# Visits of P.V over four blocks of keys with ten half tiles of P, and an order of work counted with shorter engine occupations

## The chip, the cores and the metric

The kernel runs on one core of one Trainium2 chip. The metric is the time of one execution in microseconds (us); below, a time without a unit is in us. Engines are named as in the profile: PE is TensorE (PEld its weight loads), DVE VectorE, ACT ScalarE, POOL GpSimd, SP the queue from which nearly all transfers are issued. Most executions of one kernel agree within 0.3%.

## The reference

`x` has 2048 rows of 576 values. The result is `x + s * g`, where both branches start from the normalized rows:

```python
xn = _layernorm(x)
# s: attention, 32 heads of 18 values
qkv = (xn @ wqkv).reshape(1, 2048, 3, 32, 18)
scores = einsum("bhqd,bhkd->bhqk", q, k) * 18 ** -0.5
p = softmax(scores)
s = einsum("bhqk,bhkd->bhqd", p, v).reshape(1, 2048, 576) @ wo
# g: a bilinear feed-forward part, 4608 wide, then silu
g = silu(((xn @ w_gate) * (xn @ w_up)) @ w_down)
return x + s * g
```

Everything is float32 outside; the kernel splits a float32 operand into a high and a low part and multiplies these (three products for one).

## The kernel before

There are three stages. The **prologue** (until about 205 us of the span) normalizes x, turns it into columns `xc`, and computes q, k (`qk_block`, nine blocks of 128 columns of `wqkv`) and v. The weights of a pair of blocks come by `w_load` into a raw tile and are split by `w_split`: for each block a piece of four 128-row chunks and a piece of the last 64 rows, each one ACT copy (L119) and one POOL subtraction (L121). The **end** (from about 2628 us) multiplies the attention's result by `wo` and joins the two branches, 16 tiles of 128 rows.

In between lies the **main stage**, where attention and the feed-forward part run together on PE. Most of its matmuls use half of PE's rows: the program has two streams, r = 0 in rows 0 to 63 and r = 1 in rows 64 to 127, and a matmul of one half runs beside one of the other. PE takes them in the order of the program. In each stream stand:

- `gu_op` (L630): the up (r = 0) and gate (r = 1) products of the feed-forward part, 27 matmuls of 512 columns for each 128 of its 4608 columns and each 512 rows of x: 72 units of two groups in each half, 7776 in all.
- `down_op` (L658): the product with `w_down`, 288 columns wide; 72 units of 4 times 12 matmuls in each half, 6912 in all.
- `a_item` (L534, r = 0): scores of one head for 128 queries by 512 keys; DVE takes the largest of each row (L536). 64 for each head, 2048 in all.
- `b_item` (L567, r = 1, at the end r = 0 too): the same scores again, turned over (128 keys by 512 queries) and less the maximum; ACT writes their exponentials (L569) into half of a tile `pt`. 64 for each head; the four of one block of 128 keys fill two tiles `pt` (two "half tiles" of P, 128 x 1024 each).

The product of P with V (`pv_group`, L578) uses all rows of PE and 32 of its columns for each of four matmuls. It is done in **visits**: PE leaves the two streams, does the four matmuls of each block of keys that is due, and goes back to the streams. What a visit summed in PSUM is copied by ACT (L582) on a head's first visit, and added to `oc` by DVE (L584) on the others. A head has 16 blocks of keys. After the last, `finish` turns `oc` (L594; for the last four heads PE does it, L608) and divides.

The order in which all this is written is made by a planner in Python (`order`, L973, with `visit`, `small`, `a_next`, `b_next`, `can_go`, `late`): it keeps a clock for each half of PE and a time for DVE, ACT, each PSUM bank and the transfers, and always writes down what its clocks say can go next. Its costs: 0.229 for a matmul of 512 columns, 0.131 for one of 288, 0.70 for a DVE reduction, 0.60 for an exponential, 0.858 for a block in a visit, 0.1 ahead of a visit and 0.22 behind it. A visit is asked for when `need` blocks are due (three while scores are left), and `b_ready` holds back scores that the tiles `pt` (8) have no room for (`AHEAD` = 7). `pace` spreads the scores over the stage's planned length `span`. The chip doesn't know of these numbers: it runs the written order, each engine in its own order, with semaphores where one needs another's result.

Of the kernel before, what the change touches and what calls it, by code (L numbers as in the profile page):

```python
# [40 lines left out]
def kernel(  # L41
# [51 lines left out]
    jp = consts.tile([128, 128], I32, name="jp")  # L93
    nc.gpsimd.iota(jp, pattern=[[1, 128]], base=0, channel_multiplier=-1)
    ident = consts.tile([128, 128], FT, name="ident")
    nc.vector.tensor_scalar(ident, jp, 0.0, None, op0=OP.is_equal)
# [4 lines left out]
    def w_load(srcs):  # L101

        raw = wpool.tile([128, 2, 5, 128], FT, name="wraw", bufs=2)[:, 0:len(srcs)]
        for i, (m, c0) in enumerate(srcs):
            nc.sync.dma_start(raw[:, i, 0:4, :],
                              m[0:512, c0:c0 + 128].rearrange("(k p) c -> p k c", p=128))
            for b in (0, 64):
                nc.sync.dma_start(raw[b:b + 64, i, 4, :], m[512:576, c0:c0 + 128])
        return raw

    def w_split(raw, n, pool=None):

        if pool:
            w = pool.tile([128, n, 10, 128], FR, name=f"wq{n}")
        else:
            w = wpool.tile([128, 2, 10, 128], FR, name="wgu", bufs=2)

        def piece(i, d, n, src):
            nc.scalar.activation(w[:, i, d:d + n, :], raw[:, i, src:src + n, :], AF.Copy)  # L119
            low = 4 + d if d < 8 else 9  # L120
            nc.gpsimd.tensor_tensor(w[:, i, low:low + n, :], raw[:, i, src:src + n, :],  # L121
                                    w[:, i, d:d + n, :].bitcast(FT), op=OP.subtract)

        return w, [(piece, a) for i in range(n) for a in ((i, 0, 4, 0), (i, 8, 1, 4))]
# [142 lines left out]
    ep = early.enter_context(tc.tile_pool(name="early", bufs=1, side="right"))  # L267
    vp = vstack.enter_context(tc.tile_pool(name="vp", bufs=1))
# [61 lines left out]
    def qk_block(b, c):  # L330
        w = wq[b // 2][:, b % 2]
        p = bank("a" if nqk[0] % 2 else "b", 2)
        nqk[0] += 1
        for n, (a, e) in enumerate(PAIRS):
            nc.tensor.matmul(p, w[:, a, :], xcs[c][:, e, :], start=n == 0,  # L335
                             stop=n == len(PAIRS) - 1)
# [61 lines left out]

    def w_now(i):
# [35 lines left out]
    for c in range(NCH):  # L435
# [25 lines left out]
        if c == 2:  # L461
            w_now(4)
# [690 lines left out]
```

## Time and profile before

| | us |
|---|---|
| median of 3 runs | 2706.16 (2703.46 to 2708.2) |
| the profiled execution, its time | 2705.18 |
| the profiled execution, its span | 2703.4 |
| PE busy in the span | 2654.6 |
| PE weight loads busy | 2130.2 |
| DVE busy | 1975.9 |
| ACT busy | 1489.9 |
| POOL busy | 452.4 |

The span runs from the first to the last instruction; the execution's time has 1.8 us more around it. Busy times of engines overlap, and a PE that is busy need not be busy in both halves of its rows. In the chain of work that ended last, PE holds 90%, transfers 5%, DVE 3%. The lines of the page and of the trace on which the argument rests are shown with it, below. In a row of the timeline stand the start, the duration, the engine, the line, the operation, the tiles written and read, the matmul's part of the array or the shapes, how many instructions the row holds, and in brackets the idle time before it with what ended it.

### The profile page before, as it was taken

What the parts mean: (1) busy time and instruction counts of PE and PEld (TensorE: products, weight loads), DVE (VectorE), ACT (ScalarE), POOL (GpSimd) and SP (SyncE); (2) the same over time, 40 slices, a digit from 0 to 9 for tenths busy, and PEclk for the clock granted to TensorE, in tenths of its full rate; (3) what the DMA queues carried; (4) which work ended last, traced back from release to release, by engine and by line L of the source; (5) the groups of instructions that cost most, each with busy time, mean ns of one, the idle gap of its engine ahead of it and who ended that gap; (6) DMA issues with size and microseconds to landing.
All of it is one profiled execution on the core that took longest, in us unless ns stands there. A gap on an engine that the chain in (4) does not pass through costs nothing.

```text
span 2703.4 us, 59095 instructions
## 1 busy us (share of the span) xinstructions
PE 2654.6 (98%) x24456; PEld 2130.2 (79%) x24456; DVE 1975.9 (73%) x3446; ACT 1489.9 (55%) x2731; POOL 452.4 (17%) x419
## 2 busy tenths in 40 slices
PE   7999999999999999999999999999999999999999
PEld 6899877777778787877778777777777787877769
DVE  7208777777777787877778788777778777877726
ACT  4222666666665555555555555555555555555662
POOL 3113333333311011111001101100001001100005
PEclk9999999999999999999999999999999999999999
DMA  6799888888875555666575555565676565565436
GB/s 214 225 286 263 244 224 217 220 221 214 233 201 168 164 164 176 181 203 181 163 196 165 171 164 160 168 176 164 151 199 159 167 167 174 160 177 164 137 138 209
DMA packets 212821, 508.63 MB, mean 188 GB/s; under 512 B 71112, under 2 KB 130888, under 8 KB 179016
## 3 DMA queue, kind: packets, MB, share of 16 engines
q1 hardware_dynamic: 209512, 493.64, 64.8%
q0 software_dynamic: 3040, 11.21, 1.1%
q8 instruction: 192, 3.15, 0.5%
q14 instruction: 77, 0.63, 0.1%
HBM read 314.05 MB, written 109.97 MB: 157 GB/s over the span
## 4 chain that ended last, share of the span: by engine, by line
PE 90%; DMA 5%; DVE 3%; issue 1%; ACT 1%; POOL 0%; SPq 0%; POOLq 0%; ACTq 0%; DVEq 0%
PE pg L630 32%; PE pg L578 16%; PE pg L658 14%; PE pa L534 12%; PE pb L567 8%; PE pg L1110 2%; PE pg L389 2%; PE pa L335 2%; DMA wd<-swd 2%; PE pb L335 2%; DMA wgu<-swg 1%; DVE mx L536 1%; DMA wop<-in_A_wo_dram 1%; DMA hs<-hs 1%; DVE xn L297 0%
## 5 line engine op out<-in xcount | busy, mean ns | idle before, releaser
L630 PE MATMUL pg<-xc,wgu 64*128 64x512 f32 x7776 | 1652.7, 392 | 6.9 <-DMA wgu<-swg 3.6
L569 ACT ACTIVATE pt<-pb 128x512 f32<-128x512 f32 x2048 | 1176.7, 596 | 727.8 <-PE pb L567 572.7
L536 DVE TENSOR_REDUCE mx<-pa 128x1 f32<-128x512 f32 x2048 | 1363.4, 685 | 181.0 <-PE pa L534 73.7
L630 PEld LDWEIGHTS pg<-xc,wgu 64*128 64x128 f32 x7776 | 1178.9, 186 | 59.8 <-issue 4.2
L658 PE MATMUL pg<-wd,hs 64*128 64x288 f32 x6816 | 1040.0, 293 | 4.5 <-DMA wd<-swd 3.4
L658 PEld LDWEIGHTS pg<-wd,hs 64*128 64x128 f32 x6816 | 973.4, 186 | 23.6 <-issue 5.2
L567 PE MATMUL pb<-qs,ks 56*128 56x512 f32 x2048 | 806.7, 409 | 7.4 <-ACT pt L569 6.5
L534 PE MATMUL pa<-ks,qs 54*128 54x512 f32 x2048 | 798.9, 403 | 0.1
L534 PEld LDWEIGHTS pa<-ks,qs 54*128 54x128 f32 x2048 | 365.6, 185 | 160.1 <-issue 125.8
L578 PE MATMUL pg<-pt,vt 128*32 128x512 f32 x4096 | 481.2, 599 | 3.7 <-DVE us L642 1.7
L646 POOL TENSOR_TENSOR hs<-us,hs 128x512 fp32r<-128x512 f32 x144 | 186.0, 1292 | 1775.6 <-ACT hs L645 1665.0
L567 PEld LDWEIGHTS pb<-qs,ks 56*128 56x128 f32 x2048 | 365.2, 185 | 25.8 <-ACT pt L569 13.1
L584 DVE TENSOR_TENSOR oc<-oc,pg 128x512 f32<-128x512 f32 x160 | 110.0, 688 | 334.3 <-PE pg L578 334.0
L578 PEld LDWEIGHTS pg<-pt,vt 128*32 128x32 f32 x4096 | 113.8, 109 | 250.9 <-issue 234.8
L686 DVE TENSOR_TENSOR acc<-acc,pg 128x288 f32<-128x288 f32 x544 | 239.9, 446 | 46.5 <-PE pg L658 38.9
L645 ACT ACTIVATE hs<-us 128x512 fp32r<-128x512 f32 x144 | 91.0, 632 | 160.7 <-DVE us L642 158.6
L210 POOL TENSOR_TENSOR wgu<-wraw,wgu 128x384 fp32r<-128x384 f32 x108 | 108.3, 1014 | 154.7 <-ACT wgu L209 147.3
L642 DVE TENSOR_TENSOR us<-pg,us 128x512 f32<-128x512 f32 x144 | 98.5, 684 | 5.8 <-PE pg L630 2.4
L635 ACT ACTIVATE us<-pg 128x512 f32<-128x512 f32 x144 | 85.6, 595 | 19.0 <-PE pg L630 16.8
L241 POOL TENSOR_TENSOR wd<-draw,wd 128x576 fp32r<-128x576 f32 x36 | 51.3, 1428 | 102.3 <-ACT wd L240 86.9
L339 DVE TENSOR_TENSOR hl<-pb,hl 128x512 fp32r<-128x512 f32 x18 | 12.4, 690 | 73.2 <-ACT hl L338 73.2
L582 ACT ACTIVATE oc<-pg 128x512 f32<-128x512 f32 x32 | 19.1, 598 | 84.7 <-PE pg L578 84.7
(102 smaller groups left out, 1071.7 us busy)
## 6 DMA issues: line engine op xcount, KB each, us to landing
wgu<-swg SPq DMA_DIRECT2D x102, 1152.0 KB
hs<-hs SPq DMA_DIRECT2D x288, 256.0 KB
wd<-swd SPq DMA_DIRECT2D x50, 1152.0 KB
swg<-wgu SPq DMA_DIRECT2D x36, 1152.0 KB
qs<-sqk SPq DMA_DIRECT2D x192, 144.0 KB
ks<-sqk SPq DMA_DIRECT2D x192, 144.0 KB
swd<-wd SPq DMA_DIRECT2D x18, 1152.0 KB
sqk<-hl SPq DMA_DIRECT2D x32, 512.0 KB
```

The source lines that it names most:

```text
L210: nc.gpsimd.tensor_tensor(w[:, 9 + b:12 + b, :], raw[:, b:b + 3, :], w[:, b:b + 3, :].bitcast(FT), op=OP.subtract)
L335: nc.tensor.matmul(p, w[:, a, :], xcs[c][:, e, :], start=n == 0, stop=n == len(PAIRS) - 1)
L534: nc.tensor.matmul(p, q[rows, t * 128:(t + 1) * 128], k[rows, c * 512:(c + 1) * 512], start=True, stop=True)
L536: nc.vector.tensor_reduce(mx[h][:, t, c:c + 1], p, axis=AX.X, op=OP.max)
L567: nc.tensor.matmul(p, k[rows, t * 128:(t + 1) * 128], q[rows, c * 512:(c + 1) * 512], start=True, stop=True)
L569: nc.scalar.activation(pt[t, c // 2][:, c % 2, :], p, AF.Exp, scale=scale)
L578: nc.tensor.matmul(p[32 * c:32 * c + 32, :], vt[h // 2][:, t, 6 * (h % 2):6 * (h % 2) + 32], pt[t, c // 2][:, c % 2, :], start=t == ts[0], ...
L584: nc.vector.tensor_tensor(oc[h], oc[h], p, op=OP.add)
L630: nc.tensor.matmul(ps, gw[n][half[r], a, :], xg[i][half[r], e, :], start=k == 0, stop=k == len(TERMS) - 1)
L646: nc.gpsimd.tensor_tensor(hj[:, 1, :], h32, hj[:, 0, :].bitcast(FT), op=OP.subtract)
L658: nc.tensor.matmul(ps[:, 0:HALF], hs[u][half[r], k, j, a, s * 128:(s + 1) * 128], dw[u][half[r], k, j, e, :], start=n == 0, stop=n == len( ...
L686: nc.vector.tensor_tensor(a, a, ps[:, 0:HALF], op=OP.add)
```

## The change

It has three parts.

**The main stage.** There are ten tiles `pt` (`HALVES`), and a visit is asked for when four blocks are due. The planner's costs change: an engine is taken as free 0.09 before its operation's result is there, so a reduction occupies DVE for 0.61 and an exponential ACT for 0.51; a block in a visit counts 0.864, and 0.40 stands behind a visit instead of 0.22; the span that sets the pace counts 0.05 for each block beside its 0.858 instead of 0.10. The room test uses HALVES itself.

**The room for two more tiles `pt`** (4096 bytes in each partition): the tiles `mx`, `m`, `mm`, `mt` have one buffer each instead of two, `rc` shares that of `m`, the integers `jp` for the identity lie in a tile of the prologue, and weight tiles shrink.

**The prologue's weights.** A pair of blocks is loaded as nine chunks, not ten: the first block whole (one piece of five chunks), the second without its last rows, which come by themselves (`w_last`, tiles `wl`) and are split into a tile of another pair. There are 13 pieces instead of 18; the number of transfers stays.

```diff
     def w_now(i):
-        wq[i], todo = w_split(raws[i], 1 if i == 4 else 2, ep if i == 2 else pp if i == 4 else None)
-        for f, a in todo:
-            f(*a)
+        at = 0
+        for b, n in WHOLE[i]:
+            w_piece(i, at, n, b, 0, raws[i][:, at:at + n, :])
+            at += n
...
+    WHOLE = {0: ((0, 5), (1, 4)), 1: ((2, 5), (3, 4)), 2: ((4, 5), (5, 4)), 3: ((6, 5), (7, 4)), 4: ((8, 5),)}
...
+    def w_piece(i, at, n, b, k0, src):
+
+        w, low = w_tile(i)
+        nc.scalar.activation(w[:, at:at + n, :], src, AF.Copy)
+        nc.gpsimd.tensor_tensor(w[:, low + at:low + at + n, :], src, w[:, at:at + n, :].bitcast(FT), op=OP.subtract)
...
+    def w_last(i, at, b):
+
+        raw = ep.tile([128, 1, 128], FT, name="wl", bufs=2)
+        w_load(raw, b, 4, 5)
+        return lambda: w_piece(i, at, 1, b, 4, raw)
...
-                mx[h] = mp.tile([128, NT, 4], FT, name="mx", bufs=2)
+                mx[h] = mp.tile([128, NT, 4], FT, name="mx", bufs=1)
...
-        pt = {}
+        pt, HALVES = {}, 10
...
-                pt[t, c // 2] = mp.tile([128, 2, 512], FT, name="pt", bufs=8)
+                pt[t, c // 2] = mp.tile([128, 2, 512], FT, name="pt", bufs=HALVES)
...
-        LEAD, MOST, AHEAD = 24, 40, 7
+        LEAD, MOST = 24, 40
...
         def engine(eng, start, length):
-            free[eng] = max(free[eng], start) + length
-            return free[eng]
+            free[eng] = max(free[eng], start) + length - 0.09
+            return free[eng] + 0.09
...
-        span = part + H * NT * (0.858 + 0.10)
+        span = part + H * NT * (0.858 + 0.05)
...
-            return nb < TOTAL and rows_done.get(h, 1e9) <= clk[r] and len(due) * 2 + (nb % 4 + 1) // 2 <= AHEAD
+            return nb < TOTAL and rows_done.get(h, 1e9) <= clk[r] and len(due) * 2 + nb % 4 // 2 + 1 <= HALVES
...
-                now += 0.858
+                now += 0.864
...
-            clk[0] = clk[1] = now + 0.22
+            clk[0] = clk[1] = now + 0.40
...
-                need = 3 if nb < TOTAL else 4 if any(heads) and not stuck[0] else 1
+                need = 4 if nb < TOTAL or any(heads) and not stuck[0] else 1
```

The planner writes another order of the whole main stage. The program before has 192 visits: 160 of three blocks and 32 of one (rows `x12` and `x4` of L578). The changed one has 130: 126 of four, one of three, two of two and one of one block; its lines are moved by 24 (L602 is its `pv_group`, L608 the addition to `oc`). The additions to `oc` on DVE go from 160 to 98.

In the first place, DVE a little past the middle of the main stage, the rows run from one addition to `oc` to the next. Before:

```order
L584 TENSOR_TENSOR oc<-oc,pg 128x512
L536 TENSOR_REDUCE mx<-pa 128x1 x3
L686 TENSOR_TENSOR acc<-acc,pg 128x288
L536 TENSOR_REDUCE mx<-pa 128x1 x3
L686 TENSOR_TENSOR acc<-acc,pg 128x288
L536 TENSOR_REDUCE mx<-pa 128x1 x7
L584 TENSOR_TENSOR oc<-oc,pg 128x512
```

Now, at a like place:

```order
L608 TENSOR_TENSOR oc<-oc,pg 128x512
L735 RECIPROCAL sil<-sil 128x144
L560 TENSOR_REDUCE mx<-pa 128x1 x7
L666 TENSOR_TENSOR us<-pg,us 128x512
L560 TENSOR_REDUCE mx<-pa 128x1 x4
L710 TENSOR_TENSOR acc<-acc,pg 128x288
L560 TENSOR_REDUCE mx<-pa 128x1 x3
L710 TENSOR_TENSOR acc<-acc,pg 128x288
L560 TENSOR_REDUCE mx<-pa 128x1 x3
L608 TENSOR_TENSOR oc<-oc,pg 128x512
```

Between two additions stood 13 reductions of scores; there are 17.

The second place is PE late in the last head's scores, where few feed-forward matmuls are left (`pb` are scores for the exponentials). Before:

```order
L578 MATMUL pg<-pt,vt 32x512 x12
L567 MATMUL pb<-qs_1149,ks_1150 128x512 x2
L658 MATMUL pg<-wd,hs 128x288 x7
L567 MATMUL pb<-qs_1149,ks_1150 128x512 x11
L578 MATMUL pg<-pt,vt 32x512 x12
```

Now, the last such stretch and what follows it, up to the end's first transposes (L1111):

```order
L591 MATMUL pb<-qs_1143,ks_1144 128x512
L682 MATMUL pg<-wd,hs 128x288 x2
L591 MATMUL pb<-qs_1143,ks_1144 128x512
L682 MATMUL pg<-wd,hs 128x288 x2
L591 MATMUL pb<-qs_1143,ks_1144 128x512 x4
L602 MATMUL pg<-pt,vt 32x512 x16
L682 MATMUL pg<-wdl,hs 128x288 x6
L632 MATMUL pb<-ident,oc 128x128 x4
L682 MATMUL pg<-wdl,hs 128x288 x90
L1111 MATMUL pb<-ident,oin 128x128 x4
```

Eleven scores stood in one row with nothing between them; now matmuls of the down product stand between the scores of that stretch, all but the last four.

The third place is PE at the end of the main stage before the change:

```order
L567 MATMUL pb<-qs_1149,ks_1150 128x512
L578 MATMUL pg<-pt,vt 32x512 x12
L567 MATMUL pb<-qs_1149,ks_1150 128x512 x2
L658 MATMUL pg<-wdl,hs 128x288 x16
L578 MATMUL pg<-pt,vt 32x512 x4
L608 MATMUL pb<-ident,oc 128x128 x4
L1087 MATMUL pb<-ident,oin 128x128 x4
```

The last visit and the last head's `finish` (L608) stood behind all feed-forward work; in the rows above, 96 matmuls of the down product (6 and 90) stand behind the last visit, 90 of them behind `finish`. Behind the last matmul of L630 there are now 19 scores, 162 down matmuls and two visits of four blocks; there were 40, 149 and five visits with 13 blocks.

More of the change, by code (lines that the diff above doesn't have):

```diff
@@ L267 @@
     ep = early.enter_context(tc.tile_pool(name="early", bufs=1, side="right"))
+    jp = ep.tile([128, 4 * 640], I32, name="jp", tag="xn", bufs=1)[:, 0:128]
+    nc.gpsimd.iota(jp, pattern=[[1, 128]], base=0, channel_multiplier=-1)
+    nc.vector.tensor_scalar(ident, jp, 0.0, None, op0=OP.is_equal)
     vp = vstack.enter_context(tc.tile_pool(name="vp", bufs=1))
@@ L334, in qk_block @@
         for n, (a, e) in enumerate(PAIRS):
-            nc.tensor.matmul(p, w[:, a, :], xcs[c][:, e, :], start=n == 0,
+            nc.tensor.matmul(p, wq[b, a], xcs[c][:, e, :], start=n == 0,
                              stop=n == len(PAIRS) - 1)
```

67 lines of the change are left out of this document (38 added, 29 removed).

## The prediction

> **What bounds the kernel now.** I read the engines' busy times first, then the span cut by stages, then the groups of instructions, then PE's timeline in the main stage and at its end.
>
> ```profile
> PE 2654.6 (98%) x24456; PEld 2130.2 (79%) x24456; DVE 1975.9 (73%) x3446; ACT 1489.9 (55%) x2731; POOL 452.4 (17%) x419
> 205.00:296.00 91.00, 89.50 (x782) 80.15 (x786) 75.68 (x125) 29.02 (x55) 35.21 (x32) 1.00 0.96 269
> 296.00:2586.00 2290.00, 2269.95 (x21833) 1794.71 (x21821) 1769.08 (x3063) 1354.89 (x2427) 335.86 (x286) 1.00 0.65 181
> 2586.00:2626.00 40.00, 38.37 (x290) 23.00 (x287) 9.56 (x19) 23.28 (x41) 1.28 (x1) 0.91 0.25 88
> ```
>
> The last three rows are stretches of the span: length, then busy time of PE, PEld, DVE, ACT and POOL, granted clock, share of the transfer engines and GB/s. From 296 to 2586 PE idles 20.0 of 2290.0. So PE bounds the main stage, and what counts is what its time is made of. A busy PE may have one half empty, so I price PE's work by places, the distance at which matmuls of one half follow each other:
>
> ```profile
> 1220.10 0.39 PE L630 MATMUL pg<-xc,wgu 64*128 64x512 f32 x1
> 1220.33 0.39 PE L630 MATMUL pg<-xc,wgu 64*128 64x512 f32 x1
> 1220.64 2.78 PE L578 MATMUL pg<-pt,vt 128*32 128x512 f32 x24
> 1223.36 0.50 PE L534 MATMUL pa<-ks,qs 54*128 54x512 f32 x1
> 1223.69 0.39 PE L534 MATMUL pa<-ks,qs 54*128 54x512 f32 x1
> 1228.09 0.42 PE L658 MATMUL pg<-wd,hs 64*128 64x288 f32 x2
> 1228.59 0.29 PE L658 MATMUL pg<-wd,hs 64*128 64x288 f32 x1
> 2506.11 1.07 PE L578 MATMUL pg<-pt,vt 128*32 128x512 f32 x8
> 2507.11 0.50 PE L534 MATMUL pa<-ks,qs 54*128 54x512 f32 x1
> ```
>
> A place of 512 columns is 0.23 (1220.10 to 1220.33); one of 288 is 0.13 (two last 0.42, one 0.29). A visit of three blocks (x24) holds PE from 1220.64 to 1223.36, 2.72; one of one block (x8) from 2506.11 to 2507.11, 1.00. So a block is (2.72 - 1.00) / 2 = 0.86, and 0.14 is left in each visit whatever its length. With both its edges the first visit takes 1223.69 - 1220.33 = 3.36; less two places (0.46) and three blocks (2.58), **a visit costs 0.32 beside its blocks**.
>
> ```profile
> L630 PE MATMUL pg<-xc,wgu 64*128 64x512 f32 x7776 | 1652.7, 392 | 6.9 <-DMA wgu<-swg 3.6 <-ACT wgu L209 1.3 <-POOL wgu L210 0.6
> L567 PE MATMUL pb<-qs,ks 56*128 56x512 f32 x2048 | 806.7, 409 | 7.4 <-ACT pt L569 6.5 <-DMA qs<-mt 0.8
> L534 PE MATMUL pa<-ks,qs 54*128 54x512 f32 x2048 | 798.9, 403 | 0.1
> L578 PE MATMUL pg<-pt,vt 128*32 128x512 f32 x4096 | 481.2, 599 | 3.7 <-DVE us L642 1.7 <-DVE acc L686 1.6 <-ACT us L635 0.4
> ```
>
> With the counts of these groups (L578's 4096 are eight records a block, as in the visits above, so 512 blocks) the main stage is: (7776 + 2048 + 2048) / 2 places of 0.23, 1365; 6912 / 2 of 0.13 (the count of the loops), 449; 512 blocks of 0.86, 440; 192 visits of 0.32, 61. Together 2316. It lasts from 205.38 (first L630) to 2628.31 (first L1087, below), 2423. So 107 are neither work nor visits: PE's idle time, halves that stand empty, and the end of the stage.
>
> **The change part by part.** *Visits.* There are 130 instead of 192, with the same 512 blocks: 62 x 0.32 = **19.8 less**. Below, only the 0.14 that the one-block visit shows inside could belong to a visit, 8.7. Above, all of the 107 but the end's 15.6 and PE's idle 23 could: (61 + 68) / 192 = 0.67 each, 42. I take 0.32, which is read from rows and not inferred from a rest. The 62 additions to `oc` that go lie on DVE, which waits for visits; no gain is counted for them.
>
> *The end of the main stage.* The rows from the last L630 on:
>
> ```profile
> 2585.34 0.39 PE L630 MATMUL pg<-xc,wgu 64*128 64x512 f32 x1
> 2599.19 0.50 PE L567 MATMUL pb<-qs,ks 56*128 56x512 f32 x2
> 2602.76 0.99 PE L567 MATMUL pb<-qs,ks 56*128 56x512 f32 x2 [0.20 <-ACT pt L569]
> 2603.94 1.28 PE L567 MATMUL pb<-qs,ks 56*128 56x512 f32 x2 [0.20 <-ACT pt L569]
> 2605.42 1.29 PE L567 MATMUL pb<-qs,ks 56*128 56x512 f32 x2 [0.19 <-ACT pt L569]
> 2607.62 4.28 PE L578 MATMUL pg<-pt,vt 128*32 128x512 f32 x24
> 2628.31 0.66 PE L1087 MATMUL pb<-ident,oin 128*128 128x128 f32 x4 [1.43 <-DMA oin<-so]
> 2608.00:2612.00 4.00, 4.00 (x26) 0.89 (x20) 0.02 (x1) 0.32 (x1) 0.00 (x0) 0.66 0.01 4
> 2604.77 1.09 ACT L569 ACTIVATE pt<-pb 128x512 f32<-128x512 f32 x2 [0.39 <-PE pb L567]
> ```
>
> From 2585.57 (the last L630's place) to 2628.31 are 42.7. The work behind it is 40 scores and 149 down matmuls, (40 x 0.23 + 149 x 0.13) / 2 = 14.3 with both halves full, 13 blocks (11.2) and 5 visits (1.6): 27.1. So 15.6 are lost: PE waits for exponentials in the run of eleven scores (2599.19 to 2607.62 for 13 x 0.23 = 3.0), one half is empty for much of the rest, the visit at 2607.62 takes 4.28 instead of 2.78, and the end's first transpose waits behind the last visit. In the new order the same stretch has 19 scores and 162 down matmuls (12.7), 8 blocks (6.9) and 2 visits (0.6): 20.2. What I expect it to lose: 14 scores and 26 down matmuls stand together with all but one in one half, (6.4 - 0.2) / 2 = 3.1; two exponentials take 1.09, so fourteen 7.6 against 6.4, 1.2; uneven halves right behind the last L630, 0.4; nothing at the end, since the 90 down matmuls behind `finish` (45 x 0.13 = 5.9) cover the load of `oin`. That is 4.7, so **10.9 less**. Bounds: 0, if as much is lost elsewhere, and 15.6.
>
> The clock in that stretch was 0.66 while PE counted as busy for all of its 4.00. The Trainium skill ("TensorE: Matmul & The Clock Gate", section "Part 1: The HAM clock gate") puts the lower clock down to an idle window of about 3.4 us. The rows show it after waits of 0.2 each, so sparse matmuls sufficed here. By the rows the new order, denser there, keeps the clock; by the rule the drop had another cause and could come back, which would add, as an estimate, 4.28 - 2.78 = 1.5 to the sum.
>
> *Shorter engine occupations in the planner.* They move reductions and exponentials closer together in the written order.
>
> ```profile
> 1230.24 0.68 DVE L642 TENSOR_TENSOR us<-pg,us 128x512 f32<-128x512 f32 x1
> 1230.84 0.68 DVE L536 TENSOR_REDUCE mx<-pa 128x1 f32<-128x512 f32 x1
> 1231.44 0.44 DVE L686 TENSOR_TENSOR acc<-acc,pg 128x288 f32<-128x288 f32 x1
> PEld pa L534 <- DVE mx L536: 15.6, 26, 0.8
> DVE oc L584 <- PE pg L578: 334.0, 156, 10.8
> ```
>
> Operations of 0.68 follow each other at 0.60, so the planned 0.61 is still not too short; the 0.70 of before left 0.09 of room at each. With it, weight loads of scores waited for DVE 26 times, 15.6. Queued behind such a score are the matmuls of both halves, since PE keeps its order. And DVE stands idle for 334.0 until a visit ends; in longer visits it idles longer but less often. I take 0 for this part: from -20 (all of PE's idle time goes) to +20 (it doubles). The transfers are as many and as large as before and took 0.65 of their engines' time from 296 on; PE waited for weights 3.6 at L630, and that stays.
>
> *The planner's 0.40 behind a visit, 0.864 and the pace* change only where work is written. Its visit is now 0.50 beside its blocks against 0.32 in the rows, so PE comes out of a visit before the plan; DVE and ACT have run dry by then and hold nothing up. 0.
>
> *Single buffers.* `mx`, `m`, `mm` and `rc` are written and read by DVE alone, in its order. `mt` is read by transfers, once a head (2423 / 32 = 76 apart); SP's queue gets no new wait ahead of another load. 0; without that distance it would be one transfer's wait for each head.
>
> *The prologue's pieces.*
>
> ```profile
> 25.19 2.58 PE L335 MATMUL pb<-xcx,wgu 128*128 128x512 f32 x10 [0.18 <-POOL wgu L121]
> 29.26 0.98 PE L318 MATMUL pg<-ident,xn 128*128 128x128 f32 x7 [1.16 <-DVE xn L297]
> ```
>
> A piece of five chunks takes POOL longer than one of four, so the wait of 0.18 grows by a few tenths. Behind it PE waits 1.16 for DVE's `xn` anyway, and takes it up: 0, or 0.5 if not.
>
> *The weights for the end* (`wos`) are fetched after the last gate product, and that now lies only some 25 before their first use (20.2 + 4.7) instead of 43.
>
> ```profile
> 2589.77 0.56 SPq L756 DMA_DIRECT2D wos<-swo  x1
> 2600.00:2608.00 8.00, 7.01 (x20) 3.10 (x22) 0.49 (x2) 6.53 (x13) 0.00 (x0) 0.74 0.02 7
> ```
>
> Issued at 2589.77, 4.2 after the last L630, they had landed by 2600 (7 GB/s from there): about 15 in all. Covered; without that, 1 for each us that the end is shorter than 15.
>
> **The sum**: 2705.2 (the profiled execution) - 19.8 - 10.9 = 2674.5. The median of the runs shown is 1.0 above that execution, so **2675**.
>
> **Rivals.**
>
> *More goes with the visits.* If halves stand empty because visits cut the streams into pieces, the 68 fall with the count too: 42 - 19.8 = 22 more, 2653. For it: the rest is there and 20 of idle time don't explain it. Against it: the planner evens the halves out ahead of a visit.
>
> *Half of it is given back.* The end gains nothing and waits take 5: 2706 - 20 + 5 = 2691. For it: a new order meets new transfers late.
>
> *Slower: PE waits for DVE's reductions.* The place is the score of r = 0, which needs a PSUM bank that DVE has read. If the room of 0.09 was what kept PE from waiting, and half of the 2048 reductions come late by half of it, 1024 x 0.045 = 46 are added: 2721. It decides from 31 / 2048 = 0.015 for each reduction. For it: DVE, busy 1769 of 2290, also idles 334 over the run until a visit ends, so between visits it is nearly full. Against it: 0.60 is under 0.61, and its work falls by 62 additions.
>
> *It does nothing.* If a visit's 0.32 is hidden, say because the streams' results are waited for anyway, only small changes are left: 2703. The rows at 1220 to 1223 speak against it: both halves start right behind the visit.
>
> **How the numbers follow.** The forecast has 0.60, with a range of its own from 2664 to 2688; more with the visits 0.13; half given back 0.11; nothing 0.05; slower 0.11. A measurement of this kernel tells 0.2% from no change, 5.4. Faster by more: 0.60 + 0.13 + 0.11 = 0.84; the same 0.05; slower 0.11. The range from 2654 to 2703 leaves out the slower case and little of the others.
>
> **What would show it.** Right: 130 visits, those of four blocks lasting 0.14 + 4 x 0.86 = 3.58; the end's first transpose near 2598 of the span (2628.3 - 30.7) and the last matmul of the up and gate products near 2573 (24.9 before it); no run of scores that wait for ACT behind it, and no clock below 1 there; PEld's wait for `mx` still near 16. Wrong: that wait, or PE's idle time from 296 on, grown by more than 20; visits whose 0.14 grows with their length; or an end of the main stage that loses more than 10 again.

## The result, and the profile after

The changed kernel takes 2716.27 (median of 7 runs), the kernel before 2708.19: a ratio of 1.0031 with an interval from 1.0019 to 1.0042. It is slower by 0.3%, where 2675 was predicted. Its profiled execution took 2716.77, 11.6 more than that of before. The engines' line of the page:

```profile
PE 2659.6 (98%) x24456; PEld 2125.0 (78%) x24456; DVE 1920.5 (71%) x3384; ACT 1483.5 (55%) x2726; POOL 451.2 (17%) x414
```

The main stage cut into windows as before (length, then busy time of PE, PEld, DVE, ACT and POOL, granted clock, share of the transfer engines, GB/s):

```profile
205.00:296.00 91.00, 87.84 (x741) 78.86 (x741) 72.73 (x119) 26.79 (x52) 34.70 (x32) 0.98 0.95 262
296.00:2586.00 2290.00, 2262.66 (x21692) 1779.46 (x21689) 1712.69 (x3000) 1345.34 (x2420) 334.98 (x286) 1.00 0.65 180
```

From 296 to 2586 PE now idles 27.3, where it idled 20.0. A visit of four blocks in the timeline:

```profile
303.71 0.39 PE L654 MATMUL pg<-xc,wgu 64*128 64x512 f32 x1
304.03 3.64 PE L602 MATMUL pg<-pt,vt 128*32 128x512 f32 x32
307.61 0.50 PE L558 MATMUL pa<-ks,qs 54*128 54x512 f32 x1
```

It holds PE for 3.58 (304.03 to 307.61), 0.14 beside four blocks of 0.86: what lies inside a visit is as predicted.

To see where the rest went I cut both traces at the visits. A **stretch** runs from the first matmul behind a visit to the next visit. Its **own time** is what the fuller half needs, if each matmul of the written order starts as soon as its half is free and those ahead of it have started (places 0.2303 and 0.1312, the 0.23 and 0.13 of the prediction more exactly). What it takes longer is called **over**. The edges of a visit (0.18 each) lie in it.

```text
                                        before    changed
to the first up product                 205.38     207.76
own time of all stretches               1848.6     1841.9
over                                     103.5      131.3
  of it in stretches over by > 1     36.8 in 15  69.2 in 31
512 blocks at 0.858                      439.3      439.3
inside the visits beside the blocks       28.4       19.8
rest, up to the end's first transpose      3.1       -0.1
the end stage                             75.1       75.0
```

Visits gained 8.6 inside and, with 62 edges of 0.18 (the prediction's 0.32 less its 0.14), 11.2 in what is over; the written order gained 6.7. Yet "over" grew by 27.8, so stalls grew by 39, and the prologue by 2.4. PE's own idle time from 296 to 2586 grew by 7.3 only: most of the 39 is one half that waits while the other runs, or work at a lower clock. What weight loads and PE waited for, over the whole span (us in total, times, longest):

```profile
PEld pa L558 <- DVE mx L560: 33.4, 104, 2.2
...
PE pa L558 <- DVE mx L560: 7.9, 11, 1.8
```

Scores wait for the reductions four times as often as before (26 times, 15.6, and 0.1 on PE itself). The largest single stall is another, in the stretch at 1187, over by 9.7. The timeline there:

```profile
1186.02 0.36 SPq L760 DMA_DIRECT2D wop<-in_A_wo_dram  x1
...
1187.51 0.60 ACT L606 ACTIVATE oc<-pg 128x512 f32<-128x512 f32 x1 [3.15 <-PE pg L602]
...
1195.55 0.68 ACT L766 ACTIVATE wop<-wop 128x576 fp32r<-128x576 f32 x1 [7.44 <-DMA wop<-in_A_wo_dram]
1196.14 1.07 ACT L593 ACTIVATE pt<-pb 128x512 f32<-128x512 f32 x2
...
1196.77 0.79 PE L591 MATMUL pb<-qs,ks 56*128 56x512 f32 x1 [7.32 <-ACT pt L593]
```

A part of `wo` is loaded (L760), and its split on ACT (`wo_high`, L766) is written early enough that ACT, which keeps its order, stands behind the load for 7.44. The exponentials stand behind ACT, and PE behind them for 7.32. The windows of that place show that it costs more than the halt:

```profile
1189.46:1196.78 7.32, 0.01 (x2) 0.01 (x2) 0.67 (x2) 1.23 (x3) 0.47 (x1) 0.78 0.84 119
1196.78:1200.60 3.82, 3.82 (x18) 3.05 (x20) 1.38 (x2) 2.04 (x5) 1.98 (x3) 0.52 0.94 388
```

Behind it PE runs for 3.82 at a mean clock of 0.52. The kernel before has the same halt at ACT; PE stands for 3.7 behind it, and the stretch, from 1269 on, is over by 7.1:

```profile
1272.04 0.68 ACT L742 ACTIVATE wop<-wop 128x576 fp32r<-128x576 f32 x1 [7.00 <-DMA wop<-in_A_wo_dram]
```

Of the next stretches of the changed kernel, those at 1397 (6.7) and 2373 (5.1) wait 2.8 each for weights by DMA, the one at 475 (4.2) 1.8 for DVE; the mean clock in them is 0.92, 0.91 and 0.90. The first stretch, from 208 on, is over by 6.2, where it was over by 2.2.

The end of the main stage, in the timeline:

```profile
2611.28 0.39 PE L654 MATMUL pg<-xc,wgu 64*128 64x512 f32 x1
...
2624.89 1.00 PE L591 MATMUL pb<-qs,ks 56*128 56x512 f32 x2
2626.07 1.00 PE L591 MATMUL pb<-qs,ks 56*128 56x512 f32 x2 [0.18 <-ACT pt L593]
2627.00 5.34 PE L602 MATMUL pg<-pt,vt 128*32 128x512 f32 x32
2632.26 0.66 PE L682 MATMUL pg<-wdl,hs 64*128 64x288 f32 x6
2633.20 0.66 PE L632 MATMUL pb<-ident,oc 128*128 128x128 f32 x4 [0.27 <-DVE oc L608]
2633.78 6.24 PE L682 MATMUL pg<-wdl,hs 64*128 64x288 f32 x90
2639.96 0.66 PE L1111 MATMUL pb<-ident,oin 128*128 128x128 f32 x4
```

From the last gate product's place (2611.51) to the first transpose are 28.5, of which 20.2 is work: 8.3 are lost, where 15.6 were. The last visit takes 5.34 instead of 3.64; its window:

```profile
2627.00:2632.30 5.30, 5.30 (x35) 1.33 (x34) 0.00 (x0) 0.70 (x2) 0.00 (x0) 0.68 0.01 2
```

### The profile page after: what moved, and what is told of

Its sections match the earlier page's. It is cut to its first block, busy times and chain, and to the rows that moved or that the text cites. A ratio compares the mean times of both kernels' runs of the same rounds, so it can differ in the third digit from the quotient of the medians.

```text
span 2715.0 us, 58960 instructions
## 1 busy us (share of the span) xinstructions
PE 2659.6 (98%) x24456; PEld 2125.0 (78%) x24456; DVE 1920.5 (71%) x3384; ACT 1483.5 (55%) x2726; POOL 451.2 (17%) x414
## 4 chain that ended last, share of the span: by engine, by line
PE 89%; DMA 4%; DVE 4%; issue 2%; POOL 1%; ACT 0%; SPq 0%; POOLq 0%; DVEq 0%; ACTq 0%
PE pg L654 31%; PE pg L602 16%; PE pg L682 13%; PE pa L558 11%; PE pb L591 8%; PE pg L1134 2%; PE pg L373 2%; PE pa L319 2%; PE pb L319 2%; DMA wgu<-swg 1%; DMA wd<-swd 1%; DVE mx L560 1%; DMA wop<-in_A_wo_dram 1%; DMA hs<-hs 0%; DVE us L666 0%
## 5 line engine op out<-in xcount | busy, mean ns | idle before, releaser
L654 PEld LDWEIGHTS pg<-xc,wgu 64*128 64x128 f32 x7776 | 1152.7, 187 | 67.1 <-issue 8.4
L682 PEld LDWEIGHTS pg<-wd,hs 64*128 64x128 f32 x6816 | 973.3, 186 | 32.5 <-issue 10.9
L558 PE MATMUL pa<-ks,qs 54*128 54x512 f32 x2048 | 820.3, 409 | 7.9 <-DVE mx L560 7.9
L591 PE MATMUL pb<-qs,ks 56*128 56x512 f32 x2048 | 816.2, 409 | 9.2 <-ACT pt L593 9.2
L558 PEld LDWEIGHTS pa<-ks,qs 54*128 54x128 f32 x2048 | 371.7, 185 | 140.1 <-issue 85.5
L602 PE MATMUL pg<-pt,vt 128*32 128x512 f32 x4096 | 468.1, 597 | 1.4 <-DVE us L666 1.4
L602 PEld LDWEIGHTS pg<-pt,vt 128*32 128x32 f32 x4096 | 120.2, 110 | 265.5 <-issue 259.2
L608 DVE TENSOR_TENSOR oc<-oc,pg 128x512 f32<-128x512 f32 x98 | 67.5, 688 | 316.4 <-PE pg L602 313.8
L659 ACT ACTIVATE us<-pg 128x512 f32<-128x512 f32 x144 | 85.8, 596 | 21.7 <-PE pg L654 19.8
```

The costliest lines, as they stand in the source:

```text
L558: nc.tensor.matmul(p, q[rows, t * 128:(t + 1) * 128], k[rows, c * 512:(c + 1) * 512], start=True, stop=True)
L591: nc.tensor.matmul(p, k[rows, t * 128:(t + 1) * 128], q[rows, c * 512:(c + 1) * 512], start=True, stop=True)
L602: nc.tensor.matmul(p[32 * c:32 * c + 32, :], vt[h // 2][:, t, 6 * (h % 2):6 * (h % 2) + 32], pt[t, c // 2][:, c % 2, :], start=t == ts[0], ...
L654: nc.tensor.matmul(ps, gw[n][half[r], a, :], xg[i][half[r], e, :], start=k == 0, stop=k == len(TERMS) - 1)
L682: nc.tensor.matmul(ps[:, 0:HALF], hs[u][half[r], k, j, a, s * 128:(s + 1) * 128], dw[u][half[r], k, j, e, :], start=n == 0, stop=n == len( ...
```

## The experiments

All runs first. "mx wait" is PEld's for `mx`, "end" runs from the last up or gate product to the first transpose at the end; both, like "own" and "over", are from the profiled execution. Ratios are to the kernel before, run on the same chip. The runs were made on several chips, on which the kernel before took 2708.2 to 2711.2, so a difference between two medians can be off by 3; "by the ratios" below means the difference of two ratios instead.

```text
run                       visits   own   over  mx wait,x    end  median  ratio (95%)
before                      192  1848.6 103.5  15.6,  26   43.0  2708.2
changed                     130  1841.9 131.3  33.4, 104   28.7  2716.3  1.0031 (1.0019, 1.0042)
e1 old order                192  1848.6 104.6  15.5,  25   42.9  2713.0  1.0013 (1.0003, 1.0023)
e2 occupation alone         192  1843.8 155.0  19.8,  51   85.2  2760.2  1.0186 (1.0173, 1.0199)
e3 occupation undone        128  1857.5 124.4   9.7,  31   38.1  2735.0  1.0095 (1.0080, 1.0110)
e4 long visits alone        128  1849.8 168.1   3.5,   9  102.7  2771.5  1.0230 (1.0217, 1.0243)
e5 three blocks             192  1844.0 118.4  30.7, 106   16.7  2716.0  1.0025 (1.0015, 1.0034)
e6 pace undone              130  1842.7 145.1  31.7, 103   76.4  2737.4  1.0100 (1.0083, 1.0116)
e7 later copy of wo         130  1841.9 120.9  33.9, 108   27.0  2707.9  0.9990 (0.9978, 1.0001)
e8 room at the bank         130  1841.2 111.1  16.6,  39   35.4  2700.6  0.9971 (0.9958, 0.9984)
e9 three with room          192  1840.4 110.6  20.2,  48   16.6  2704.6  0.9978 (0.9967, 0.9989)
e10 two blocks              257  1841.6 149.3  64.8, 185   16.7  2752.9  1.0158 (1.0140, 1.0177)
e11 slower loads            130  1848.5 102.9  14.3,  40   17.9  2692.7  0.9933 (0.9919, 0.9947)
e12 pace alone              192  1848.3 102.3  18.0,  26   19.6  2707.3  0.9988 (0.9977, 0.9999)
e13 other order, four       130  1842.4 139.7  32.7, 100   28.8  2729.6  1.0071 (1.0052, 1.0090)
e14 other order, three      192  1845.3 160.2  31.7, 104   16.4  2753.6  1.0162 (1.0144, 1.0180)
e15 other order, before     192  1851.5 110.9  16.1,  25   51.2  2721.2  1.0044 (1.0029, 1.0060)
e16 three, best             192  1847.6 114.0  24.3,  55   16.4  2715.0  1.0013 (1.0005, 1.0022)
e17 best, other order       130  1848.3  99.2  13.8,  40   16.5  2694.6  0.9936 (0.9915, 0.9957)
e18 later copy in before    192  1849.0  94.4  19.9,  28   51.0  2701.6  0.9966 (0.9955, 0.9978)
```

### The parts one by one

**e1**, the changed kernel with every cost and `need` of before, and so with the order of PE's matmuls of before in the main stage:

```diff
-            free[eng] = max(free[eng], start) + length - 0.09
-            return free[eng] + 0.09
+            free[eng] = max(free[eng], start) + length
+            return free[eng]
-        span = part + H * NT * (0.858 + 0.05)
+        span = part + H * NT * (0.858 + 0.10)
-                now += 0.864
+                now += 0.858
-            clk[0] = clk[1] = now + 0.40
+            clk[0] = clk[1] = now + 0.22
-                need = 4 if nb < TOTAL or any(heads) and not stuck[0] else 1
+                need = 3 if nb < TOTAL else 4 if any(heads) and not stuck[0] else 1
```

> All of the change but its order: new prologue, ten tiles pt, single buffers, with visits of three and every cost of the planner as before, which gives the order of PE's matmuls of before. If the prologue's pieces cost what the two traces differ by at the first up product (207.76 - 205.38), the run is 2.4 slower than before, about 2710.5, and its excess over the streams' own places in the main stage stays at 103. If single buffers or the tiles cost something, the main stage from the first to the last L654 grows beyond 2380. If neither costs anything, 2708.

Measured: 3.6 slower than before (0.8 to 6.2), first up product at 207.68, own time the same, "over" 104.6. So ten tiles and single buffers cost nothing that shows, and the prologue costs what it does in the changed kernel. The rows before (DVE and POOL, while the second block of x is normalized; the last two are means of POOL's pieces by their shape, 23.8 to 30.7):

```profile
23.84 3.82 POOL L121 TENSOR_TENSOR wgu<-wraw,wgu 128x512 fp32r<-128x512 f32 x4 [10.58 <-DMA xin<-in_A_x_dram]
...
25.49 0.33 DVE L299 COPY xn<-xn 128x64 f32<-128x64 f32 x1
...
29.24 0.33 DVE L299 COPY xn<-xn 128x64 f32<-128x64 f32 x1
...
L121 POOL TENSOR_TENSOR wgu<-wraw,wgu 128x512 fp32r<-128x512 f32 x2 | 2.6, 1292 | 10.6 <-DMA xin<-in_A_x_dram 10.6
L121 POOL TENSOR_TENSOR wgu<-wraw,wgu 128x128 fp32r<-128x128 f32 x2 | 1.4, 680 | 0.0
```

and in the changed kernel (the last two again by shape, 23.2 to 30.4):

```profile
22.87 0.20 DVE L284 COPY xn<-xn 128x64 f32<-128x64 f32 x1
...
23.30 3.12 POOL L399 TENSOR_TENSOR wgu<-wraw,wgu 128x640 fp32r<-128x640 f32 x2 [10.78 <-DMA xin<-in_A_x_dram]
...
23.79 1.43 DVE L284 COPY xn<-xn 128x64 f32<-128x64 f32 x1
...
28.91 1.15 DVE L284 COPY xn<-xn 128x64 f32<-128x64 f32 x1
...
32.63 0.76 PE L303 MATMUL pg<-ident,xn 128*128 128x128 f32 x4 [2.06 <-DVE xcx L307]
33.05 4.59 PE L319 MATMUL pa<-xcx,wgu 128*128 128x512 f32 x12
...
L399 POOL TENSOR_TENSOR wgu<-wraw,wgu 128x640 fp32r<-128x640 f32 x1 | 1.9, 1872 | 10.8 <-DMA xin<-in_A_x_dram 10.8
L399 POOL TENSOR_TENSOR wq<-wraw,wq 128x512 fp32r<-128x512 f32 x1 | 1.5, 1489 | 0.0
```

A copy of 64 columns takes 0.20 alone. In the kernel before POOL's long pieces (1.29) alternate with short ones (0.68), and in the trace the three slower copies meet short ones and take 0.33 or 0.34. In the changed kernel two copies meet long pieces, one of five chunks (1.87) and one of four (1.49), take 1.43 and 1.15, and end 0.06 behind these pieces. The Trainium skill ("SBUF — State Buffer", section "SBUF: two separate sides") says that a DVE operation in a two-port mode and a POOL operation share a port pair, that the one that starts first has it for its whole instruction, and that the other waits; these rows agree. From the first of the block's normalizations to the last copy's end DVE takes 7.80, where it took 6.65, and PE's wait for `xcx` grows from 1.24 to 2.06. Behind that wait twelve matmuls take 4.59: from 32 to 42 the mean clock is 0.83. That spell came in six of the fifteen profiles with the new prologue (first up product at 207.7 to 208.8, otherwise at 206.5 to 207.0) and in none of the five with the old one (204.6 to 205.5).

**e2**, the kernel before with the shorter occupation alone:

```diff
-            free[eng] = max(free[eng], start) + length
-            return free[eng]
+            free[eng] = max(free[eng], start) + length - 0.09
+            return free[eng] + 0.09
```

> The kernel before with one edit: an engine counts as free 0.09 before its result is there. Theory A (the room of 0.09 kept PE from waiting for DVE and ACT): slower than before by 20 to 50, 2728 to 2758, with PEld's wait for mx from 15.6 to over 30 and the share of scores that start within 0.1 of the reduction that frees their bank from 1.2% to some 8%. Theory B (the 0.40 behind a visit, with 0.32 in the rows, is what costs: the plan counts on time that PE does not take): within 5 of before, 2703 to 2713, since the 0.22 stands. Theory C (long visits lose by themselves what they save): also within 5.

Slower by 51, just above theory A's range, but only a small part of it for theory A's reason: the wait for `mx` grew by 4.2. "Over" grew by 51.5, of which 31 lies before the last gate product. There PE waited 10.3 for `wgu` by DMA instead of 3.6, and three stretches (over by 8.8, 7.9, 7.1) have ACT's halt at `wop`, where the kernel before has one. Another 20 lies behind the last gate product: the end went from 43.0 to 85.2, in part because 83 scores and 23 blocks stand in it instead of 40 and 13. Its window:

```profile
2596.20:2681.40 85.20, 78.15 (x421) 37.09 (x420) 13.07 (x25) 48.44 (x90) 1.30 (x1) 0.82 0.16 54
```

Scores without feed-forward matmuls beside them wait for ACT, and the mean clock is 0.82. A planner that counts shorter occupations writes the feed-forward part faster, while `pace` still holds the scores back to the old span. That is read from the code; e6 and e12 measure the pace.

**e3**, the changed kernel with the occupation of before (the first four lines of e1's diff):

> The changed kernel with the planner's occupations of before (0.70 and 0.60), everything else as changed; 128 visits of four blocks. Theory A: the excess in the stretches between visits falls from 131 to about 100 and the wait of PEld for mx to 16; but the written order leaves its halves less even (the fuller half of the stretches sums to 1857.5 places' time against 1841.9), which gives 15 back: about 2716 - 31 + 15 = 2700. Theory B: the excess stays at 131, so 2716 + 15 = 2731. Theory C: as B.

2735, near theory B's number, and its excess of 124 lies between the 100 and the 131 of the theories. The wait for `mx` did fall, from 33.4 to 9.7, as theory A says. But the halves became less even (15.6), the end 9.4 longer, and PE waited 5.3 for pieces of `wgu` that ACT and POOL split too late. In this kernel the shorter occupation is worth 19 (17 by the ratios), though its waits cost.

**e4**, only the longer visits (e1's diff without its last two lines):

> Only the longer visits: four blocks, ten tiles, with all costs and the pace of the planner as before; 128 visits, fuller halves 1849.8 (before 1848.6). Theory A and theory B both: the visits' saving shows in full, 64 x 0.32 = 20 less, and the prologue's 2.4 more: 2708 - 20 + 2 = 2690. Theory C (the saving is lost to longer stretches whatever the costs): 2705 to 2716, with an excess of 120 to 135 in the stretches.

2771: none of the theories. Against e1, which has the same costs and visits of three, the longer visits lose 58. "Over" is 63.5 above e1's: 37 of it lies behind the last gate product, where with the old pace 104 scores stand in an end of 102.7. The other 26 lies before it, although 64 edges (11.5) are gone there. PE waits there 18.3 for `wd`, `wgu` and `xc` by DMA, where e1 waits 6.3, and 8.9 for pieces of `wgu` that ACT and POOL split, where e1 waits 1.9; the wait for `mx` is only 3.5. So longer visits can bring stalls that have nothing to do with the reductions.

**e5**, the changed kernel with visits of three:

```diff
-                need = 4 if nb < TOTAL or any(heads) and not stuck[0] else 1
+                need = 3 if nb < TOTAL else 4 if any(heads) and not stuck[0] else 1
```

> The changed kernel with one edit: a visit is asked for at three due blocks, so 192 visits instead of 130, with every cost, the pace and the prologue as changed. Theory D (the visits' saving arrives in full and what eats it comes from the costs): 62 x 0.32 = 20 more than the changed kernel, 2736, with an excess in the stretches that is larger by the edges of 62 visits (0.18 each, 11). Theory C (longer visits bring stalls that eat what they save): 2716 or less, since fewer stretches longer than 1 us over their own places remain, and no score stands behind the last gate product any more (19 did).

2716.0 against 2716.3: the fourth block brought nothing here. Its 62 more visits cost 8.3 inside and 11 in edges, but the stretches over by more than 1 hold 21.8 instead of 69.2. The wait for `mx` is the same, so it does not come from the fourth block. The occupation alone (e2) has 19.8 and its undoing (e3) 9.7: the wait comes from the occupation together with the other new costs, which were not parted further.

**e6**, the changed kernel with the pace of before:

```diff
-        span = part + H * NT * (0.858 + 0.05)
+        span = part + H * NT * (0.858 + 0.10)
```

> The changed kernel with one edit: the span that sets the pace of the scores counts 0.10 for each block again, not 0.05. 75 scores and 22 blocks then stand behind the last gate product, against 19 and 8. As predicted for this edit (only the place of the work changes): 2716. Theory E (the pace sets the length of the end, where scores that have no feed-forward matmuls beside them go at ACT's speed): the stretch from the last gate product to the first transpose took 85 with 83 scores where only the occupation was changed, 28.7 with 19, so 0.88 for each score: 49 more there, of which 20 is work that has left the part before (56 scores, 14 blocks, 4 visits), so 29 more in all, about 2745.

21 slower (19 by the ratios), with an end of 76.4 and, behind the last gate product, 21 more "over": theory E, a little under its 29. The edit that I had costed at nothing is worth 21 here.

**e12**, the kernel before with the new pace alone (the reverse edit):

> The kernel before with one edit: 0.05 for each block in the span that sets the pace, not 0.10. 5 scores and 4 blocks are left behind the last gate product, against 40 and 13. Theory E (the pace sets the end's length): the end's 15.6 of loss shrink to 3 to 6, so 2709 - 11 = 2698; the occupation and the visits stay, so the wait for mx stays near 16 and the stretches' loss before the last gate product near 97. As predicted for this edit: 2709.

The end falls from 43.0 to 19.6, and 13 blocks and 40 scores become 4 and 5, but the time falls by only 0.1% (0.0 to 0.2), 3 instead of 11: PE's waits for `wgu` by DMA rose from 3.6 to 13.6. With the occupation of before, the old pace cost little.

### The stalls

**e7**, the changed kernel with a pause behind the load of `wo`:

```diff
-        PAUSES = {"wo_low": 16.0, "last": 16.0}
+        PAUSES = {"wo_low": 16.0, "last": 16.0, "wo_load": 16.0}
```

> The changed kernel with one edit: after the load of a part of wo the planner lets 16 us pass, not 6, before it writes ACT's copy of it. In the changed kernel ACT stood 7.4 behind that load at 1187, PE 7.3 behind ACT, and the stretch took 9.7 over its places, the largest of all. Theory F (stalls from a chance meeting of loads and queues, each with a spell of lower clock behind it, are a good part of what was lost): 7 to 9 less than the changed kernel, 2708, and no stretch near 1187 with an excess over 2. Rival: the time is taken up by what waits next (the reductions that stood behind the same halt): 2714 to 2717.

8.3 less (11 by the ratios), as theory F says, and no halt of ACT at `wop` is left. In every one of the thirteen kernels without this edit ACT waits there, for 3.7 to 25.2 in all; of the seven with it e9 alone does, for 2.4.

**e18**, the same edit in the kernel before:

> The kernel before with the later copy of wo alone. The halt at 1268 cost 7.1 over its places: 7 less. 49 scores stand behind the last gate product instead of 40: 9 x 0.23 / 2 are moved there, and by 0.88 for each score at the end, less the work that left the part before, 5 more at most. 2702 to 2708. No stretch between 1100 and 1300 should lose over 3.

0.34% faster than before (0.22 to 0.45), some 9: a little more than its halt, although the end grew by 8. The stretches before the last gate product that are over by more than 1 hold 21.5 instead of 32.1.

**e8**, as e7, with room at the bank of a reduced score:

```diff
-            banks["a"][slot] = engine("DVE", clk[r] + 0.45, 0.70) + 0.06
+            banks["a"][slot] = engine("DVE", clk[r] + 0.45, 0.70) + 0.18
```

> As the one before, and the planner counts the bank of a reduced score as free 0.18 behind the result instead of 0.06: the shorter occupation stays, PE alone gets room. Theory A (waits for DVE's reductions are what the shorter occupation cost): PEld's wait for mx falls from 33.4 in 104 waits to under 15, and the time to 18 less than with the later copy alone, about 2690, less what nine more scores at the end take back (28 behind the last gate product instead of 19, 4 by the places and the blocks): 2694. Rival (DVE is full between visits, so its waits only move): the wait for mx stays above 25 and the time within 4 of the later copy alone.

The wait for `mx` halves:

```profile
PEld pa L558 <- DVE mx L560: 16.6, 39, 2.6
```

and the time falls by 7.3 more, half of what was expected; the end took back 8.4 (27.0 to 35.4, where 4 were counted). That is theory A's mechanism at half its size.

**e11**, as e8, with slower transfers in the plan:

```diff
-            queue[0] = max(queue[0], start) + size / 0.24
-            return queue[0] + 2.0
+            queue[0] = max(queue[0], start) + size / 0.22
+            return queue[0] + 3.0
```

> The run with room at the bank, and the planner counts transfers as slower (0.22 instead of 0.24 for the bytes, 3.0 instead of 2.0 behind them). Theory G (what is left of the long stretches' loss is PE's waits for wgu, wd and xc, 11.5 there, with a spell of lower clock behind those over 2): these waits fall below 5 and the stretches over 1 us lose 25 instead of 47; the fuller halves sum to 1848.5 instead of 1841.2, which takes 7 back, and 3 scores are left at the end instead of 28: 2700 - 22 + 7 - 5 = 2680. Rival (the loads come late because of what the chip's queue does, not the plan): waits stay over 9, 2703 to 2708.

2692.7, 0.67% faster than before (0.53 to 0.81). But theory G's reason is not borne out: PE still waits 14.0 for `wd`, `wgu` and `xc`, 6.8 of it at one place, while stretches over by more than 1 hold 38.8 instead of 47.2 and the end lost 17.5 of its length.

### Three blocks or four, and the scatter of orders

**e9**, e8 with visits of three (e5's diff added):

> The run with room at the bank (2700.6), but a visit is asked for at three due blocks: 192 visits, no score behind the last gate product. Theory C (four-block visits eat with stalls what they save): the wait for mx halves here as there (30.7 to 15), the halt at the copy of wo goes, 8 and 15 less than the changed kernel with visits of three (2716): 2693 to 2700. Theory D (with the stalls for mx gone, the longer visits pay): 2700 + 20 less the end's 4 to 8: 2712 to 2716.

4.0 slower than e8 by the medians, 2 by the ratios, whose intervals overlap: between the two theories, and not clear of the noise.

**e10**, the changed kernel with `need` = 2:

> The changed kernel with a visit asked for at two due blocks: 257 visits instead of 130 (192 with three). If a visit costs 0.32 and shorter visits bring no fewer stalls than those of three (22 in 9 stretches over 1 us, against 69 in 31 with four), this is 65 x 0.32 = 21 slower than with three: 2737. If the stalls still fall with the length of the visits (theory C as a steady rule), at most those 22 can go: 2715 to 2720. The wait of PEld for mx stays near 31 in both, since the occupation is the same.

37 slower than with three. 21 of it is the visits' price; the wait for `mx` doubled to 64.8, which neither theory had. Below three blocks the saving of longer visits is plain.

**e13, e14, e15**: the changed kernel, e5 and the kernel before in another order of the same costs:

```diff
-        PACE, SKEW, PULL, FIRST, ROWS = 1.01, 5.2, 3.0, 5.0, 6.0
+        PACE, SKEW, PULL, FIRST, ROWS = 1.01, 5.25, 3.0, 5.0, 6.0
```

> The changed kernel with SKEW at 5.25 instead of 5.2, which shifts by 0.05 how far one stream may lead the other and so gives another order with the same costs (fuller halves 1842.4, 20 scores at the end, 130 visits). If the time belongs to the costs: within 4 of the changed kernel, 2712 to 2720. If single stalls set it (the halt at wo of 9.7 and the late loads at 1397 and 2373 of 6.7 and 5.1 are met or not): anywhere from 2698 to 2720.

> The changed kernel with visits of three blocks and SKEW at 5.25 (fuller halves 1845.3, no scores at the end, 192 visits). Theory C (what longer visits save is eaten as a rule): within 5 of the run before this one. Theory H (it was chance, the visits' 20 is there in the mean): 10 to 20 slower than the run before this one.

> The kernel before with SKEW at 5.25 (fuller halves 1851.5, 49 scores and 13 blocks at the end instead of 40). By the costs: 3 for the halves and 5 for the end more than before, 2715 to 2720. If single stalls set it: 2700 to 2725.

An edit that should not matter moved the three by 13, 38 and 11; e13 and e14 lie outside what was expected of them. ACT's longest halt in e14 (timeline of ACT), and then its waits at `wop` over the span (us in total, times, longest):

```profile
1121.51 0.68 ACT L766 ACTIVATE wop<-wop 128x576 fp32r<-128x576 f32 x1 [10.52 <-DMA wop<-in_A_wo_dram]
```

```profile
ACT wop L766 <- DMA wop<-in_A_wo_dram: 25.2, 4, 10.5
```

Three stretches with that halt are over by 10.7, 10.3 and 8.6, where e5 had one of 8.2. The wait for `mx`, in contrast, is the same in each pair of orders (32.7 and 33.4, 31.7 and 30.7, 16.1 and 15.6). Four blocks are 24.0 faster than three in this pair.

**e16**, e11 with visits of three, and **e17**, e11 with SKEW at 5.25:

> The best setting so far (room at the bank, slower transfers in the plan, later copy of wo; 2692.7 with 130 visits of four blocks) with visits of three (192; fuller halves 1847.6 against 1848.5). Theory C: 2690 to 2697. Theory H (the saving of 20 arrives where the stalls are out of the way): 2705 to 2713.

> The best kernel so far (four blocks, room at the bank, slower transfers in the plan, later copy of wo; 2692.7) with SKEW at 5.25: other order, same costs; fuller halves 1848.3 against 1848.5, no scores behind the last gate product (3 there). If the time is its costs': 2690 to 2700. If it was a lucky order: 2703 to 2716, as the scatter of 11 to 38 in the other pairs would allow.

e16 is 22.3 slower than e11 (their runs, 2710.4 to 2716.5 and 2691.5 to 2697.6, don't overlap), 2 above theory H's range and far from theory C's. e17 lies 1.8 from e11, so the best kernel's time is not that of one lucky order; in this one pair, without ACT's halt, another order moves little. e11 and e17 are the best found, and faster than both kernels.

## Why the prediction was wrong

- **Fewer visits, 19.8 less.** What was seen of the price was right: 0.15 inside each, with counts of 130, 192 and 257. The step that failed is the sum: it took off the visits and the end's gain and left the rest of the 107, some 91 of empty halves and idle time, as it was. That belongs to the written order, and a new order has its own: here stalls grew by 39, more than the 30.7 that was forecast as gain. Five pairs at equal costs give the fourth block's worth: -58 (e4, old costs and pace), 0 (e5), 4 (e9, not clear of the noise), 22 (e16) and 24 (e14). With 0.18 taken off for each visit, "over" is larger with four blocks by 75, 24, 12, 0 and -9. So the saving of the visits stood against stalls that were as large or larger in two orders, and not in all. Why was not settled. Of the 39 here, the halt at `wop` and the waits for `mx` are shown by e7 and e8 (8.3 and 7.3, and the kernel before had a halt and waits of its own); the rest was not assigned.
- **Shorter occupations, 0.** Mis-sized, and without a size of its own: alone they cost 51 (e2), and undoing them in the changed kernel costs 19 (e3). The wait for `mx` went from 15.6 to 33.4, and every kernel with the new occupation, 0.864 and 0.40 and no room has 30.7 or more; room at the bank gave 7.3 back. The rival "slower: PE waits for DVE's reductions" named place and mechanism, at 46 instead of this; that its 2721 lies near the measured time is luck. My argument against it, 0.60 under 0.61, told only that DVE keeps up, not that its result lies ready when the score comes.
- **The pace and the 0.40, 0.** Failed for the pace: 21 in the changed kernel, 3 in that of before. It decides how many scores are left without cover. The 0.40 and 0.864 were not tried alone.
- **The end, 10.9 less.** Mis-sized: a loss of 15.6 became 8.3 and not 4.7, so 7.3 were gained. I held that the denser order keeps the clock; its mean fell to 0.68 in the last visit, and that cost 1.7. Another 1.1 goes around the last head's transposes (2632.26 to 2633.78, with 0.39 of matmuls), which I gave nothing. (14 scores and 25 down matmuls are 6.5 by my places and not 6.4, which moves nothing.) The rule of the Trainium skill that I weighed ("TensorE: Matmul & The Clock Gate", "Part 1: The HAM clock gate") would not have told it either: in the 3.41 ahead of it PE counts as busy for 3.21 (rows in the last section).
- **The prologue, 0.** Wrong by 2.3, the means of the fifteen and the five profiles: I costed POOL's longer pieces at PE's wait for them, and not at DVE's copies that meet them.
- **Single buffers, `wos`, 0.** Right: e1's main stage has before's own time and an excess 1.1 larger, and no wait of PE for `wos` stands in the changed kernel's trace.
- **Not seen at all:** ACT's halt at `wop`, 7.1 in the kernel before and in its trace. I took it for idle time that stays; it is a place at which ACT waits 3.7 to 25.2 in each of thirteen kernels, and its size changes with the order.

## What to carry to other kernels

Where a planner writes the order, a few us gained by one cost are less than what another order of the same costs can do (11, 13 and 38 in three pairs here, 2 in a fourth): try two or three orders of each before you judge, and sum a change only with the stalls counted as unknown. Look through the long stalls of the trace one by one first; a copy that an in-order engine meets before its load has landed cost 7 to 11 at a time, and one line took it away. A cost that is shortened in a plan takes room from whatever waits for that result, and can move more uncovered work to the end: change the pace with it.

## What the runs showed of the hardware

The granted clock is 1.00 or 0.50 in all twenty traces; the means between come of spells at 0.50 that last 3.41 or a multiple of it (but for those that the end of a run cuts). Windows of the changed kernel around two such spells:

```profile
1412.04:1415.45 3.41, 1.05 (x12) 1.05 (x14) 0.07 (x1) 0.85 (x2) 0.73 (x1) 1.00 1.04 377
1415.45:1418.86 3.41, 3.41 (x23) 3.28 (x20) 1.84 (x3) 1.20 (x2) 0.00 (x0) 0.50 0.77 172
1418.87:1422.28 3.41, 3.41 (x34) 0.94 (x32) 0.00 (x0) 0.00 (x0) 0.00 (x0) 1.00 0.61 142
...
2623.78:2627.19 3.41, 3.21 (x16) 1.75 (x18) 0.46 (x1) 3.16 (x7) 0.00 (x0) 1.00 0.56 224
2627.19:2630.60 3.41, 3.41 (x20) 0.87 (x16) 0.00 (x0) 0.51 (x2) 0.00 (x0) 0.50 0.01 1
```

No halt of 3.41 was needed: PE was busy for 1.05 of the 3.41 ahead of the spell at 1415, for 0.95 and 1.64 ahead of those at 2385 and 487, and for 3.21, with 16 sparse matmuls, ahead of the last visit's. At half the clock a spell of 3.41 costs up to 1.7 of work, an estimate, so a stall can cost more than its length: the stretches at 1397 and 2373, with one wait of 2.8 each (and 0.7 of small ones at 1397) and a spell each, are over by 6.7 and 5.1. A DVE copy of 0.20 took 1.43 beside a long piece of POOL's subtraction and 0.33 beside a short one, so which pieces it meets decides how late DVE's small work comes.
